# One order string for another: a recurrent attention block and a hard-swish layer on one core

## The chip, the cores and the metric

One core of a Trainium2 chip (trn2). The metric is the device time of one execution in microseconds. The engines are named as the profile names them: PE (TensorE, matrix products; PEld are its weight loads), DVE (VectorE), ACT (ScalarE), POOL (GpSimd) and SP (SyncE, which here issues nearly all DMAs).

## The reference

Two blocks behind each other. The first is a linear recurrence with 4 batches, 8 heads, 768 steps and head size 48; the second takes its result as 3072 tokens of width 384.

```
for t in range(S):
    cur = einsum('bhd,bhe->bhde', u * k[t], v[t])
    y[t] = einsum('bhd,bhde->bhe', r[t], state + cur)
    state = w[t][..., None] * state + einsum('bhd,bhe->bhde', k[t], v[t])
x = y.transpose(0, 2, 1, 3).reshape(3072, 384)
h = x @ w_in                              # 384 -> 2048
g = h * clip(h + 3, 0, 6) / 6
out = g @ w_out                           # 2048 -> 384
```

The weights `moe_w_in` and `moe_w_out` come as 64-bit floats and are turned into 32-bit ones on the chip.

## The kernel before

The sequence is cut into 24 chunks of 128 steps. Per chunk i, two scans on DVE (`back{i}`, `fore{i}`) make running products of the decay w; `K{i}` and `R{i}` scale k and r by them (on DVE for the first seven chunks, on POOL after); `own{i}`, `sum{i}` and `diag{i}` make the diagonal part with u (by PE's `dot{i}` for chunks below 9; from 9 on by two POOL multiplies, the second with u's broadcast over 128 partitions, and a DVE sum). `score{i}` multiplies K and R on PE, `above{i}` puts the causal half into A on DVE, `kv{i}` and `kvs{i}` make the new part of the state, `decay`, `mid`, `decb` and `state` update it on DVE, and `read{i}` gives the chunk's output, which `leave{i}` copies on ACT and `move` sets in place by DMA.

Four chunks make a block of 512 tokens; there are six. Block 0 runs its first product in plain form: `up0.f.c` on PE, `ramp` on ACT, `gate` on DVE. Meanwhile the weights are converted (`fetch` on SP, `low` and `sign` on ACT, `shift` and `full` on DVE) and the sums of weights for a scheme with fewer products are made on DVE (`sin`, `sout`). Blocks 1 to 5 use that scheme: sums of the input (`tx`), `up{b}.{d}.{r}` on PE, `read{b}...` on ACT and DVE, `clip`, `gate`. The second product of every block is done per half p as seven products `down{b}.{p}.{k}` in two parts each, with sums of g (`sum{b}.{p}`) ahead of them and reads of the banks (`out{b}.{p}.s1`, `u`, `v`, `c11`, `c12`, `c21`, `c22`) behind or between them, then `store`. Through blocks 1 to 5 the weights are fetched again and looked over (`refetch`, `vet`) for a flag at the end.

Everything is a step of a `Plan`: a name, an engine, a duration, what it comes after, the buffers that it holds. The order in which the steps are emitted, and so each engine's queue, is read from a string `ORDER`: two characters per step, its rank. The tile framework adds the waits that the data and buffers need; engines work off their queues in that order.

```
rank = [CODE.index(ORDER[2 * i]) * 64 + CODE.index(ORDER[2 * i + 1]) for i in range(len(steps))]
out = [n for _, n in sorted(zip(rank, steps))]
```

The plan also computes a start for each step from its durations. Its only use in the emitted program: where a PE step is to start later than PE would be free (in the first 60 us), `emit` puts filler matmuls (`spin`, L1276) in front of it; four more stand at the very beginning.

Other names of the profile: L397 is `fetch`, L354, L361 and L356 are the chunk loads (chunk 0 in two parts: `feat0`, `later`), L368 `tok` (v), L364 `u`, L373 `rkt` (r and k by token, from chunk 9), L713 `move`, L542 `flip` (a transposing DMA of K), L755 `store`, L434 and L438 `back`, L443 `fore`, L454 `K`, L458 `R`, L467 and L470 `own`, L479 `dot`, L739 `up0`, L840 `up` of the other blocks, L897 `down`, L917 the DVE reads of the banks, L816 `sout`, L787 to L791 `sin` and `tx`, L882 `sum`, L706 `leave`.

Of the kernel before, what the change touches and what calls it, by code (L numbers as in the profile page):

```python
# [81 lines left out]
ORDER = (
    "AEAIAHASATAVAKANAOAPAQARAbAjAXAYAZAaAhApAdAoAyA4A7AGALAeAmAiAsAlAWAcAtAuAvA+BCAwAxA8A9BDBPBHBIBMBdBiAfBhA1BKBNBQA6A2"
    "BEBFBJBpBzB0BLBVBnB1CBCJCLCNCeCkAgBYBTBlB7CKBfBRBoBtB4CaChCnB+CACSCWCMCpCrDYC3C5DTDBBjCOBwCsCqCtB3ByCHCfDJDLDUDfC7DD"
    "DRD0D3EDEIEPEVEzB5EUC6DMDaDgDIDADPDXEEEWEcDcD1EoEKFBFJFaFTFwHZG5CgFSDvECEvExD4ELElEyFPFQFhEhFmFWFrF0F/GmG1EXGUEmFiGD"
    "GRFZFbFjFlFvGHGtGFGMGbGpG9HBHFHKHcHdHfHxFRGfGSGZGzG7GYFnF4F9G6HeHtGkGlGoH9HSH/IBIgI1JqFUHMFVGjGuHjH5GnIXIoI+I/JBG4HY"
    "H7JcJsJtJuJvKkK4LELKHaKaJKH+JUJYKSJNJMJQKBKHLMJfKAKOKlKgKnKvLSLiHbK6HiJZKXK8LGJ5KbKuKzLILXK0K+LHLhLNLtLuLyL2MOL9IUJ+"
    "KeKyLYLkLqLBLmLnLsMBMCLeLfLgMdMeMfMuNQLCL7MRLzMFL5L/L1MjMmMxMyMzMGMUMYM7NCNDNwN3PyPvLdNTL8MpM+M6NZM0MqMrNLNkN5NNNRNn"
    "ONNqOQObOxO+PcM/NEN0NMNWNzOCNPOHOUPDPOPbNXN2OAPaO7PdPfPhPjQDQMQKNSOpOeNxOGPHPNN6PMPsP+P/QCO0PCPERWQ+RXRlRvRyScN1Q0PI"
    "PiP4QAQzP1QyQ3RPRQR2QBQIQnR5RFR7R8SQS/TmUBUCPlRxPwQiQxSASzQsRMRbTCTDTGSBSTSpTfS5TiTjTqT4UMQ4SISKRJSlTPTSRVSnSqTWTXUJ"  # L90
    "S7TITdUGTLUOUSUVUZUaUdUeSVTyTZTATsUDUPTNT+UXUoUpU3TtT6UAVQVRVZVaVdVoWuUQU6URUcUuUrVjUsUmUtUxVsVvU4U5VMVzVbV2WQWhW/Xe"
    "YMX1U0WXVHVIVkWPW+VKVlV7WNWfXFWZWzW0XZWGXbXrX3YJU7VrXaWHW2XTXhWkXfXmXpX2X7XHXOXYX+XMYBYCYWYeYxYjBgAFAJAkAnAqAzBWCTCU"
    "BcCbAMA0A5ArA/BXBZBmBrB2A3BABBBOBUCPCwCxCoDFAAABADACAUBkBvCEB6CRDrD7EOEQEaDCDlDnDwDyETEfEiEkE2E8E9FEE/FFFDFLFMFHFXB8"
    "CdDdC/DiD+EdEeEZErC+DWDjDmD/BSBaBbDpDtDxDqDzD2BGBeBsCCCcCiFAFOFgCjClCuDQDVDZEbEpEwC1C2C8CvCyCzEAEHEJCDCVCZE+FGFIDHDK"
    "DOESEYEnCXCYCmDsD5D6EMENERD9EFEGBqBuBxFpFuGLB/CFCQF7F8GODSDeDhEtE3E4DuD8EBEqEuE0B9CGCIEgEjEsDbDkDoE5E6E7C0C4DEGNGXGc"
    "C9DGDNGdGiGxFeFyF3GPGTGsG8G+HDHEHIHNHOHPHRHTHUHhHkHqHrHzH3H6IAIHIIILIPIeIhIiIkInIrI2I3I4I5I6I7JAFdFfFkFqGVGgF2GBE1GA"
    "FzF+FYGCF1GKFCFKFsFtFcFoF5F6GGGQGIGJGhGqFNFxGEGWGeGaG2HXIEGrHLG/HQGyHgHJHlGwG0GvHAHHHmHGHVHuHvHoHpH0H1G3HCHWHnHwHsH8"
    "IVINHyH2H4IJIKIbIpIyJSIZIlIxICISIsIDIMIYIGITIcIvIwI9IRIdIjIFIqIaImIuIQIOJEI8IWItIfIzI0JHJVJgJhJ0J7JGJXKiKjJkJ6LTLUJC"
    "JDJLJPJFJTJnJ1KKJpJxKCJaJbJ2JJJWJmJRJeJzJ/J4KGJIJlJoJOJrJwJyJ9JiJdKDKLJjKIJ3KJKFKPKQKRKUKhKoKVKWLDLWKEKMKtK/KNKTKsLA"
    "J8K3KfK1KcKdKwK9KZKmKYKpKrLFKxK2LQLRLLLOLZLaKqK5K7LJLvLPLrOfL+LVL4LwL6LjMELxMJLbLlLcLpMHMML3MAMIMNMKMLMbMhLoL0MDMPMa"  # L100
    "MVMkNAOgMQMSMcM8MlMvM3NJNgM5NFNcM4NaNlMTMiMsMWMgMwNGNKNdMtM2NfMZNIM1M9NHMnMXNUNeMoNmNBNbNVNhNjNuOIOLOYNoNyOMOnNYNiPr"
    "PtNONpPJPVN/OFOTOjOvOEOROlODOJOqNsN4N8NrN9OPOdOXOoOBOOOZNtOcOKOWOaN7NvOkOmN+OwOSOhOiOyOzO3O4PnPoOuO2PqP2OtO1PKPkOrOs"
    "P0P5OVO6PFPRO8PBPLPeO5O/O9PGPPPTPQPSPWPgPYPZPxPzPAPUPXP8PpPmQVT7TJP3QUQGQYP6QLQJQpP7P9QFQHQOQRQPQQQlQqQWQXQjQkQNQTQS"
    "QeQ5QhQmQ6SJQZQaQbQcQuQ/RERSRhRCRHRUR+R/ShQdQvQ8QfQwRBRLRGRYQ2RASSQtRRQ9RKRNQ1QgRTRaQ7SoRDRZRORgRqR3SDSCSYRdRkTHTURo"
    "RpTQTRRsR4TnTvRmRzR9SOSgSLSRSmStSuS0RfRnR1RcRtR0SUSPSaRuR6SyRiSNSFSGSZRrReSWSrRwS+SMSbSXSfSjSkSxT2T5S1S2TkTrSiSsTxTz"
    "SdSeTYTgSESHS9TOS3TMTBThSwS4SvS6TTTVTETFTbTuTcTeT3T9S8TKTaTlT1TpT/W7X0TwT0UNUhULUWUYUiUEUFUIUUUTUjUfUgUwU1UlUnUyUzUH"
    "UbUkUqU+UvU/VqWyU8U9VSVpVBVVVhVxWFWdWeWwVNVOVWVAVEVGVCVUVeVuVtV5VLVXVTVDVwVPVgWmVFVJWBWxVYVcVfV4V1V6WbXPXQWJWiX5X6Vn"
    "V3WaWcWIWKXqXyViV0V9WEWYW3XIXAXBXdWTWWWsV8WDWRVyWAWVWnWqW4WCWUWjV/WlWSWpXUWMV+XGXiWOWtWgWoWrW8XkXoYHXCXEYKYXW1W9YDYE"
    "XJXKYIYQWvW5YOYVYYY/YZYkYlYqYPYgYUYiYsYtYoYpZAZCYuYvY7Y9YhY5YrY4ZMY6ZEaFZxW6XVXcXwXLXsXgX4XRXSXWXXXnYFXtXuX8X9YRYSYa"
    "YbXjXlXvYGYmYTYfYwZwZTaEYzY0Y1Y2ZGZPZeZlZzZZZbZkaiala+Y3ZHZNY8ZJZQZiZhZnZKZSa2ZDZfZOZcZdZIZFZrZqZLbYZWZjZmZuZ0Z5aLau"  # L110
    "bAZ8aVbdbfaPaUbQbSZgZ1bHbPZRZ2aIaQagaHaOaXaxa5bRZyZ7Z6ZoaKaRafaYakZaZ4bDZ3aJZ+aNaSZ/Z9aTacaMbbaWahaZanaparasbmbnaeaj"
    "bcbpaoaqa3a/aaabbGbLadazawbEatbFbBbOaya4ama7a8bMa9bCbZbgbVbWbhbia6bUbKbTb8bXbtcEb9cDbubjbobsb+brbybxb1bkbqblbwb2b4bz"
    "b0cAcBb5b/cIcKbvb7b3b6cHcCcMcGcJcFcNQoQrZVZXToUKZpaAYyZBXNYAZUZYX/YcXzYNRIRjPuQEZsaBYnY+aDavT8U2YLYdaCa0ZtZvaGa1VmWL"
    "bIbJXDXxbNbabecL"
)
# [1509 lines left out]
```

## Time and profile before

| what | value |
|---|---|
| median of 3 runs | 528.02 us (526.06 to 531.23) |
| profiled execution | 528.87 us, its span 527.1 us |
| mean granted PE clock | 0.997 |
| PE busy | 517.7 us, 98% |
| DVE, ACT, POOL busy | 431.6, 290.1, 86.7 us |
| filler matmuls (L1276) | 94 instructions, 15.6 us |
| DMA | 70.33 MB, mean 133 GB/s |

Matmul ends are modelled and matmuls overlap, so the distance from one start to the next says more than a duration. A bracket behind a row gives the idle time of the engine before it and what ended it. A row of a stretch gives the busy time of each engine in it, with the count of instructions.

### The profile page before, as it was taken

The numbers are of one execution on the slowest core, as the hardware profiler recorded it, in microseconds if no ns is written. First come the engines' busy times: TensorE is split into PE (matmuls) and PEld (weight loads), VectorE is DVE, ScalarE is ACT, GpSimd is POOL, SyncE is SP. The second block draws the span as 40 slices with busy tenths as digits, with TensorE's granted clock in tenths as the row PEclk, the third lists the DMA queues.
The fourth block names the chain that finished last, engine by engine and source line by source line (L and its number), as shares of the span: only waits on it lengthen the run. The fifth ranks groups of instructions, "written<-read, shape, count | busy, mean of one in ns | idle before, by whom it ended". The sixth has DMA issues, their size and how long they took to land.

```text
span 527.1 us, 13608 instructions
## 1 busy us (share of the span) xinstructions
PE 517.7 (98%) x5642; PEld 477.7 (91%) x5642; DVE 431.6 (82%) x762; ACT 290.1 (55%) x680; POOL 86.7 (16%) x79
## 2 busy tenths in 40 slices
...
GB/s 329 329 275 182 234 285 92 49 53 181 150 3 63 54 172 68 96 206 72 109 99 101 150 10 130 140 101 106 265 33 153 101 151 203 131 199 136 60 10 57
DMA packets 37235, 70.33 MB, mean 133 GB/s; under 512 B 19088, under 2 KB 27184, under 8 KB 37168
## 3 DMA queue, kind: packets, MB, share of 16 engines
...
q8 instruction: 46, 0.75, 0.6%
...
q10 hardware_dynamic: 128, 0.00, 0.0%
HBM read 59.69 MB, written 4.72 MB: 122 GB/s over the span
## 4 chain that ended last, share of the span: by engine, by line
PE 86%; DVE 6%; DMA 3%; SPq 2%; ACT 1%; issue 1%; DVEq 0%
PE bank L897 29%; PE bank L840 28%; PE bank L739 8%; PE bankS L897 5%; PE bankS L840 5%; PE y_ps L598 2%; PE bank L504 2%; PE y_ps L607 2%; PE y_ps L620 2%; DMA feat_in<-in_feat_dram 1%; PE bankS L1276 1%; PE ps L479 1%; DMA bits<-in_moe_w_in_dram 1%; SPq L713 1%; DVE E L434 1%
## 5 line engine op out<-in xcount | busy, mean ns | idle before, releaser
L861 ACT ACTIVATE clip<-g,three 128x512 f32<-128x512 f32 x80 | 56.1, 719 | 49.0 <-DVE g L857 27.8
L857 DVE TENSOR_TENSOR g<-bank,g 128x512 f32<-128x512 f32 x80 | 53.4, 684 | 26.2 <-PE bank L840 23.1
L897 PE MATMUL bank<-w_out,g 128*128 128x192 f32 x384 | 67.3, 327 | 0.0
L897 PEld LDWEIGHTS bank<-w_out,g 128*128 128x128 f32 x384 | 63.2, 190 | 0.5
L865 DVE SCALAR_TENSOR_TENSOR g<-clip,g 128x512 f32<-128x512 f32 x80 | 59.1, 754 | 4.0 <-ACT clip L861 3.9
L495 ACT ACTIVATE A<-eyes,dg 128x64 f32<-128x64 f32 x192 | 49.8, 338 | 0.5 <-DVE dg L487 0.3
L454 POOL TENSOR_TENSOR K<-feat_in,E 112x512 f32<-112x512 f32 x17 | 25.0, 1469 | 146.0 <-DVE E L434 82.8
L855 ACT COPY g<-bank 128x512 f32<-128x512 f32 x50 | 28.8, 585 | 33.5 <-PE bank L840 32.3
L739 PE MATMUL bank<-xT,w_in 128*128 128x256 f32 (+1 forms) x216 | 46.7, 366 | 0.0
L739 PEld LDWEIGHTS bank<-xT,w_in 128*128 128x128 f32 x216 | 37.4, 194 | 4.5 <-issue 0.3
L458 POOL TENSOR_TENSOR W<-feat_in,W 112x512 f32<-112x512 f32 x17 | 25.3, 1490 | 94.4 <-DVE W L443 80.9
L840 PE MATMUL bank<-xT,w_in 128*128 128x256 f32 x160 | 40.1, 379 | 0.0
L706 ACT COPY xT<-y_ps 48x256 f32<-48x256 f32 x88 | 32.2, 365 | 10.4 <-PE y_ps L607 9.6
L915 ACT ACTIVATE o<-bank 128x192 f32<-128x192 f32 x36 | 11.5, 327 | 47.1 <-PE bank L897 47.0
L897 PE MATMUL bankS<-w_out,g 128*128 128x192 f32 x192 | 34.9, 328 | 0.0
L897 PE MATMUL bank<-more,g 128*128 128x192 f32 x192 | 34.4, 329 | 0.1
L840 PEld LDWEIGHTS bank<-xT,w_in 128*128 128x128 f32 x160 | 30.2, 190 | 3.8
L897 PEld LDWEIGHTS bank<-more,g 128*128 128x128 f32 x192 | 31.4, 190 | 1.1 <-DVE o L917 0.5
L434 DVE TENSOR_TENSOR_SCAN E<-feat_in,back 112x520 f32<-112x520 f32 x24 | 29.9, 1245 | 2.8 <-DMA feat_in<-in_feat_dram 2.8
L470 POOL TENSOR_TENSOR rk<-rk_in 128x384 f32<-128x384 f32 x15 | 17.5, 1164 | 88.9 <-DMA kvs<-rk 39.4
L897 PEld LDWEIGHTS bankS<-w_out,g 128*128 128x128 f32 x192 | 31.6, 190 | 0.2
L840 PE MATMUL bank<-xT,bits 128*128 128x256 f32 x120 | 30.7, 380 | 0.8 <-DMA xT<-xT 0.8
...
## 6 DMA issues: line engine op xcount, KB each, us to landing
...
bits<-in_moe_w_in_dram SPq DMA_DIRECT2D x8, 768.0 KB, 7.3
bits<-in_moe_w_out_dram SPq DMA_DIRECT2D x8, 768.0 KB, 5.6
feat_in<-in_moe_w_in_dram SPq DMA_DIRECT2D x8, 768.0 KB, 4.8
feat_in<-in_moe_w_out_dram SPq DMA_DIRECT2D x8, 768.0 KB, 4.5
...
v_in<-in_tok_dram SPq DMA_DIRECT2D x24, 192.0 KB, 4.4
feat_in<-in_wflat_dram SPq DMA_DIRECT2D x6, 768.0 KB, 4.7
```

The source lines that it names most:

```text
L434: nc.vector.tensor_tensor_scan(out=E_[:, ::-1], data0=d["w"][:, :0:-1], data1=back.rearrange("q p t -> q (p t)")[:, ::-1], initial=0.0, op ...
L454: early(i).tensor_mul(d["K"], d["k"], d["E"][:, :, 1:])
L458: early(i).tensor_mul(d["R"], d["r"], d["R"])
L495: nc.scalar.activation(out=d["A"][:, h, :], in_=eyes, func=ACT.Copy, scale=d["dg"][:, h])
L706: nc.scalar.copy(out=blocks[bk]["xT"][g * GP:g * GP + D, :, at:at + HL], in_=st[i]["y_ps"][a][(g ^ a) * GP:(g ^ a) * GP + D, :, :])
L739: nc.tensor.matmul(h_ps[:, :(c1 - c0) * L], lhsT=w_in[:, f // 2, j, f % 2, :], rhs=b["xT"][:, j, c0 * L:c1 * L], start=(j == 0), stop=(j = ...
L840: nc.tensor.matmul(b["p", d, c][:, z * HB:(z + 1) * HB], lhsT=weight(W_PLACE[r], d)[:, z, :], rhs=x_at(bk, X_PLACE[r]), start=fresh and z ...
L855: nc.scalar.copy(out=out_, in_=src)
L857: nc.vector.tensor_tensor(out=out_, in0=src, in1=out_of(bk, d, other), op=ALU.add if sign > 0 else ALU.subtract)
L861: nc.scalar.activation(out=c, in_=out_of(bk, d, u), func=ACT.Relu, bias=three, scale=twice)
L865: nc.vector.scalar_tensor_tensor(out=g, in0=blocks[bk]["r", d, u], scalar=6.0, in1=g, op0=ALU.min, op1=ALU.mult)
L897: nc.tensor.matmul(b["d", p, to][:, :h], lhsT=a, rhs=w(), start=(f == 0 and k in (1, 5)), stop=(f == HF - 1 and k in (2, 3, 4)), skip_grou ...
```

## The change

The string `ORDER` is replaced by another of the same length, a permutation of the same 1806 steps (459 on PE, 666 on DVE, 460 on ACT, 49 on POOL, 172 on SP). No step is added, taken away or altered, and no duration in the plan's table. The count of fillers follows from the order: 42 steps of two instructions instead of 47. What the reader will need of the two queues:

```
SP before    fetch6 feat0 later feat1 tok0 fetch0 tok1 fetch2 feat2 feat3 fetch4 fetch1 fetch3 tok3 u tok2 feat4 fetch7 ...
SP after     feat0 later feat1 tok0 fetch6 feat2 tok1 fetch0 fetch4 fetch3 feat3 tok2 fetch5 feat4 fetch1 fetch7 tok3 ...
             ... feat9 feat10 move1.0.1 move1.0.0 u rkt9 flip8 store0.0 move1.1.1 move1.1.0 ...

PE before    dot0 turn0 kv0 score0 dot1 clear0 first0 turn1 read0 kv1 score1 dot2 up0.1.0 clear1 first1 ...
             ... up0.15.2 down0.0.4.0 read6 down0.0.4.1 down0.1.5.0 down0.1.1.0 down0.1.1.1 down0.1.5.1
             down0.1.6.0 down0.1.2.0 down0.1.6.1 read7 (7 down steps) up1.0.12 up1.0.1 ...
PE after     dot0 turn0 kv0 dot1 turn1 score0 clear0 score1 kv1 dot2 first0 clear1 first1 turn2 read0 score2 read1 ...
             ... read6 down0.1.1.0 down0.1.1.1 down0.0.4.0 down0.1.2.0 down0.0.4.1 down0.1.5.0 down0.1.5.1
             read7 (9 down steps) up1.0.1 up1.0.9 ...

DVE before   ... sin0.4 sout4.0 out0.0.c22 gate0.14.2 out0.0.c12 ... tx1.0 ... sum9 ...
DVE after    ... out0.0.c12 sin0.7 sout4.0 sin0.8 sout4.1 sum0.1.1.0 fore8 out0.0.c22 sin0.9 above7 sin0.10 sum9
             sin0.11 ... sin0.20 sin1.0 tx1.0 ...

POOL before  K7 R7 K8 K9 R8 R9 own9 own10 ...
POOL after   K7 K8 R7 own9 R8 K9 R9 own10 ...
```

The diff, cut to its first lines (it goes on so through the whole string):

```diff
 ORDER = (
-    "AEAIAHASATAVAKANAOAPAQARAbAjAXAYAZAaAhApAdAoAyA4A7AGALAeAmAiAsAlAWAcAtAuAvA+BCAwAxA8A9BDBPBHBIBMBdBiAfBhA1BKBNBQA6A2"
...
+    "AAAIABAKALAZACAEAFAGAQAXAmArANAPATAUAWAcAnAwA/BIBZAHASAMAeAVAkAYARAaAdAgAlAoA9AfAjAsAxA5BBAyBABHBQBcAOBSAuA8BCBJA1Aq"
...
 )
```

More of the change, by code (lines that the diff above doesn't have):

```diff
@@ L82 @@
 ORDER = (
-    "AEAIAHASATAVAKANAOAPAQARAbAjAXAYAZAaAhApAdAoAyA4A7AGALAeAmAiAsAlAWAcAtAuAvA+BCAwAxA8A9BDBPBHBIBMBdBiAfBhA1BKBNBQA6A2"
-    "BEBFBJBpBzB0BLBVBnB1CBCJCLCNCeCkAgBYBTBlB7CKBfBRBoBtB4CaChCnB+CACSCWCMCpCrDYC3C5DTDBBjCOBwCsCqCtB3ByCHCfDJDLDUDfC7DD"
-    "DRD0D3EDEIEPEVEzB5EUC6DMDaDgDIDADPDXEEEWEcDcD1EoEKFBFJFaFTFwHZG5CgFSDvECEvExD4ELElEyFPFQFhEhFmFWFrF0F/GmG1EXGUEmFiGD"
-    "GRFZFbFjFlFvGHGtGFGMGbGpG9HBHFHKHcHdHfHxFRGfGSGZGzG7GYFnF4F9G6HeHtGkGlGoH9HSH/IBIgI1JqFUHMFVGjGuHjH5GnIXIoI+I/JBG4HY"
@@ L87 @@
[L87 to L111, printed above, removed]
@@ L112 @@
-    "bcbpaoaqa3a/aaabbGbLadazawbEatbFbBbOaya4ama7a8bMa9bCbZbgbVbWbhbia6bUbKbTb8bXbtcEb9cDbubjbobsb+brbybxb1bkbqblbwb2b4bz"
-    "b0cAcBb5b/cIcKbvb7b3b6cHcCcMcGcJcFcNQoQrZVZXToUKZpaAYyZBXNYAZUZYX/YcXzYNRIRjPuQEZsaBYnY+aDavT8U2YLYdaCa0ZtZvaGa1VmWL"
-    "bIbJXDXxbNbabecL"
+    "AAAIABAKALAZACAEAFAGAQAXAmArANAPATAUAWAcAnAwA/BIBZAHASAMAeAVAkAYARAaAdAgAlAoA9AfAjAsAxA5BBAyBABHBQBcAOBSAuA8BCBJA1Aq"
+    "AvA3A+BGBPBRBEBNBbBgBDBqByCnB+CRBKCMBTBwBiBsBkBLBVBmCICiCkCoB9CBCbCsCpC1C5DpC9DIDXDaBXCPCKC+CWC4CdCCCGCUClDTDnDqDGDS"
```

30 lines of the change are left out of this document (added).

## The prediction

> **What bounds the kernel now.** I read the page's parts 1 and 2 first, then stretches, waits, and the engines' rows in order of time.
>
> ```profile
> PE 517.7 (98%) x5642; PEld 477.7 (91%) x5642; DVE 431.6 (82%) x762; ACT 290.1 (55%) x680; POOL 86.7 (16%) x79
> ```
>
> PE is busy 98% of the span, but "busy" counts filler matmuls and half-speed ones. The stretches (columns: stretch, length, then busy us and count of PE, PEld, DVE, ACT, POOL, then granted clock, DMA share, GB/s):
>
> ```profile
> 0.00:8.33 8.33, 5.97 (x28) 5.78 (x28) 4.72 (x12) 3.32 (x4) 3.01 (x15) 1.00 0.75 279
> 5.66:30.00 24.34, 22.20 (x422) 20.36 (x421) 23.82 (x40) 20.70 (x57) 0.00 (x0) 1.00 0.93 356
> 30.00:60.00 30.00, 29.75 (x466) 25.48 (x459) 25.38 (x53) 24.77 (x63) 0.00 (x0) 0.94 0.57 202
> 60.00:95.00 35.00, 35.00 (x456) 30.96 (x456) 33.83 (x67) 28.05 (x67) 1.18 (x1) 1.00 0.57 195
> 95.00:129.50 34.50, 34.50 (x440) 33.11 (x439) 32.66 (x60) 16.05 (x40) 9.95 (x7) 1.00 0.37 98
> 129.50:132.83 3.33, 2.49 (x16) 2.19 (x15) 0.00 (x0) 0.70 (x2) 0.00 (x0) 1.00 0.47 156
> 134.78:523.75 388.97, 388.77 (x3836) 360.99 (x3836) 311.95 (x534) 198.21 (x450) 72.51 (x56) 1.00 0.36 111
> ```
>
> From 134.78 to 523.75 PE idles 0.20 us. No order can gain more than crumbs there, since both orders hold the same matmuls. So the case is block 0, up to 134.78. There DVE is as full as PE: it idles 0.52 + 4.62 + 1.17 + 1.84 + 3.33 = 11.5 us of the 127.2 from its first wait on data (5.66) to the first sum of block 1 (132.83), so 115.7 us are work. What PE lost in block 0 (the second fence line is the filler alone, by stretches of its source line: PE, PEld, clock, DMA, GB/s):
>
> ```profile
> 8.33 0.63 PE L479 MATMUL ps<-u_col,rk 112*64 112x2 f32 x16 [0.93 <-DVE rk L467]
> 8.33:60.00 51.67, 9.67 (x66) 8.61 (x66) 0.97 0.72 264
> 29.52 0.57 PE L620 MATMUL y_ps<-v_in,kn 64*48 64x48 f32 x32 [1.03 <-ACT xT L689]
> 30.77:34.18 3.41, 3.41 (x12) 2.81 (x11) 1.22 (x2) 0.67 (x4) 0.00 (x0) 0.50 0.99 403
> 132.52 1.10 PE L840 MATMUL bank<-xT,bits 128*128 128x256 f32 x4 [0.84 <-DMA xT<-xT]
> 134.78 1.10 PE L840 MATMUL bank<-T__1844,bits 128*128 128x256 f32 x4 [1.16 <-DVE T__1844 L787]
> ```
>
> The first real matmul comes at 8.33; filler takes 9.67 us after it; PE idles 1.03 at 28.5; a 3.41 us stretch runs at half clock (1.7 us of work lost); and at the seam to block 1 it waits 0.84 and 1.16.
>
> **Part by part.** The diff exchanges one order string: the same 1806 steps, durations unchanged. I decoded both strings into each engine's queue and matched the trace's instructions to the steps, so every step has a measured length (its start to the next start). Filler is placed by the planner: 47 filler steps before (94 instructions), 42 after; 10 instead of 14 ahead of the first real matmul, 32 instead of 33 behind it.
>
> **1, the start.** SP's first issues were a weight fetch, then chunk 0's decay part, then its rest; now the fetch stands behind chunk 1 and its v. (Issues, their times to landing, and the DVE instructions that they release:)
>
> ```profile
> 0.81 0.40 SPq L397 DMA_DIRECT2D bits<-in_moe_w_in_dram  x1
> 1.27 0.41 SPq L354 DMA_DIRECT2D feat_in<-in_feat_dram  x1
> 1.73 0.43 SPq L361 DMA_DIRECT2D feat_in<-in_feat_dram  x1
> bits<-in_moe_w_in_dram SPq DMA_DIRECT2D x1, 768.0 KB, 4.8
> feat_in<-in_feat_dram SPq DMA_DIRECT2D x1, 260.5 KB, 4.8
> feat_in<-in_feat_dram SPq DMA_DIRECT2D x1, 512.0 KB, 5.8
> 6.21 1.24 DVE L434 TENSOR_TENSOR_SCAN E<-feat_in,back 112x520 f32<-112x520 f32 x1
> 7.61 0.67 DVE L467 TENSOR_TENSOR rk<-feat_in 112x512 f32<-112x512 f32 x1
> ```
>
> Landings at 5.6, 6.1 and 7.5: after the first, 772 KB in 1.9 us, 400 KB/us. Issued first, chunk 0's 260 KB land (768 - 260) / 400 = 1.3 us sooner than the fetch did, at 4.35, and the rest at 5.7. DVE begins near 4.45 instead of 5.66: **1.2 us**; the first real matmul comes near 6.6. Bounds: 0 to 1.7.
>
> **2, the u broadcast and the order of fetches.** (Issue, times to landing of the v before it and of u, and DVE's wait:)
>
> ```profile
> 21.48 0.60 SPq L368 DMA_DIRECT2D v_in<-in_tok_dram  x1
> 22.12 0.43 SPq L364 DMA_DIRECT2D u_bc<-in_ub_dram  x1
> v_in<-in_tok_dram SPq DMA_DIRECT2D x1, 192.0 KB, 4.4
> u_bc<-in_ub_dram SPq DMA_DIRECT2D x1, 192.0 KB, 6.7
> 33.03 1.24 DVE L434 TENSOR_TENSOR_SCAN E<-feat_in,back 112x520 f32<-112x520 f32 x1 [2.19 <-DMA feat_in<-in_feat_dram]
> ```
>
> The v landed at 25.9, u at 28.8: 192 KB held the stream 2.9 us, against 0.5 at 400 KB/us. Chunk 4 stood behind u and six fetches. Now it stands behind five, and u behind block 1's first moves. By the landing chain chunk 4 comes near 27 instead of 33, so DVE's 2.19 goes. Next late there: the second score, which reaches PE near 24.5, behind six fillers (some 0.7 us of DVE idle). I followed PE, DVE and ACT through the first 30 us by hand with the rows' lengths: the step that ended at 34.5 (the one at half clock) ends near 29.8, with equal work done; DVE, idle 5.1 us to 60 before, should idle about 2.2. So DVE gains 1.2 + 2.9 = **4.1**, and PE, which from 60 on is tied to DVE by gates and sums (part 3), the same. Bounds: 1.5 (ACT, 83% busy from 30 to 60, paces DVE) to 5.5.
>
> **3, a new wait behind block 0's seventh output half.** The step `down0.0.4.0` must wait for `out0.0.c22`, which reads its bank. (DVE's c22; PE's `up0.15.2`, then `down0.0.4.0`:)
>
> ```profile
> 105.50 0.34 DVE L917 SCALAR_TENSOR_TENSOR o<-bank,o 128x192 f32<-128x192 f32 x1
> 104.82 1.46 PE L739 MATMUL bank<-xT,w_in 128*128 128x256 f32 x6
> 106.11 1.46 PE L897 MATMUL bank<-more,g 128*128 128x192 f32 x8
> ```
>
> Before, c22 started at 105.50 after 93.6 us of DVE work (steps added up, from 0), so DVE ran 11.9 behind its work; down0.0.4.0 started at 106.11 after 83.6 us of PE work, 22.5 behind. The difference of **10.6** hardly moves from 60 on, as each engine waits for the other when it does. Now c22 comes after 100.8 us, down0.0.4.0 after 88.1: with c22's 0.27 and 0.15 to get there, the difference must be 13.1. PE would arrive 2.5 us early; behind it wait all of block 0's remaining matmuls, and DVE's sum of `down0.1.5.1` then waits 2 us for PE. Some of PE's usual small gaps vanish in that wait: net **1.8 lost**. [...]
>
> **4, GpSimd in the busy stretch.** `own9` (two instructions) ran while DVE idled; now it stands ahead of R8, near 105, when DVE is full. (POOL and DVE rows:)
>
> ```profile
> 103.31 1.44 POOL L454 TENSOR_TENSOR K<-feat_in,E 112x512 f32<-112x512 f32 x1 [1.57 <-DVE E L434]
> 103.63 1.94 DVE L816 TENSOR_TENSOR more<-w_out,top 128x768 f32<-128x768 f32 x1
> 126.33 1.18 POOL L470 TENSOR_TENSOR rk<-rk_in 128x384 f32<-128x384 f32 x1
> 89.26 0.95 DVE L816 TENSOR_TENSOR top<-w_out,bits 128x768 f32<-128x768 f32 x1
> ```
>
> A sum that takes 0.95 elsewhere (last row) took 1.94 beside a POOL multiply: it ended 0.8 after that multiply's end, 104.75. So each POOL instruction can cost DVE up to 1; two here, 0 to 2, of which the K multiplies, moved to earlier places, give about 1 back at c22. [...]
>
> **5, the seam to block 1.** Its first sum needs read7's outputs moved by DMA. Before, 7 matmul steps of 1.30 us followed read7, now 9: 2.6 us more cover for copy, moves and sums, against 0.84 + 1.16 us of waits and 0.4 around them. They go: **2.4 gained** (bounds 0.5 to 2.5).
>
> **6, behind.** In block 1 one gate stands 0.7 us too late for `down1.0.1.1` (queue positions); blocks 2 to 5 have the old margins. **0.6 lost** (0 to 1.2).
>
> Sum: -4.1 + 1.8 - 2.4 + 0.6 = **-4.1**, on the profiled 528.87 (span 527.1 and 1.8 around it): 524.8. The median shown is 528.02, 0.85 lower, its runs 526.06 to 531.23. I forecast 528.0 - 4.1, rounded: **524.0**.
>
> **Rivals.** [...]
>
> *Given back*: ACT and DVE hold each other through two clip buffers from 30 to 60, so part 2 gives 1.5, and PE falls to half clock once (1.7, of which 1.0 hides behind DVE): -1.5 + 1.8 - 2.4 + 0.6 + 0.7, near 527.2. The row for the clock: PE idled 1.03 us in the 3.4 before 30.77 and half clock followed; filler is thinner now. [...]
>
> *Slower: u comes too late.* u is issued only when leave5 has let two moves go, then rkt9; own9 waits for both, R8 waits behind own9 on POOL, read7 needs R8, and DVE's `sum9` now stands ahead of half of block 1's weight sums. (A leave's four copies, and one move's three issues:)
>
> ```profile
> 122.42 1.51 ACT L706 COPY xT<-y_ps 48x256 f32<-48x256 f32 x4 [1.64 <-PE y_ps L607]
> 52.16 1.87 SPq L713 DMA_DIRECT2D xT<-xT  x3
> ```
>
> The value copy ahead of leave5 on ACT waits for down0.0.5.1, which ends after 74.5 us of PE work, near 92.7; plus 1.5, plus two moves, u is issued near 98.5 and lands 5 to 6.7 later, near 104; rkt9 1 us behind; own9 (2.2) ends near 107. sum9's turn is at 102.4 us of DVE work, near 111. From 112 every microsecond of lateness is one of span; from 116 the kernel is slower than before; at 120 it takes 532. Against: it needs 9 us of error.
>
> **How the numbers follow.** Forecast 524.0: 0.47 (522.7 to 525.8). All arrives, 521: 0.24. Given back, 527.2: 0.22. Slower, 530 and more: 0.07. Range 520.3 to 528.2, leaving out some 0.06 below and 0.1 above. One per cent is 5.3 us, about what a measurement can tell. Faster by over 1% is under 522.7: 0.24 and a little of the forecast's, 0.28. Slower by over 1%: 0.04. Within: 0.68.
>
> **What would show it.** The first scan near 4.5 and first L479 near 6.6; no 2.19 wait of DVE on feat_in near 30; clock 1.0 there; a PE wait on `o` or a DVE gap of about 2 us near 107 to 117; no wait on xT or T at the seam, block 1's first sums' matmuls near 130 instead of 134.8; from there to the end 389 us again. Wrong if sum9 waits for POOL, or DVE's idle time to 60 stays near 5.

## The result, and the profile after

The changed kernel takes 526.06 us (median of 22 runs, 521.57 to 528.43) against 528.29 for the one before (526.06 to 531.31): a ratio of 0.9946, 95% interval 0.9925 to 0.9967. The forecast was 524.0. The profiled execution took 525.09, 3.8 below the profiled one of before, where the sum said 4.1. Several of the sum's terms were wrong, though, by up to 2.4 us, and they cancel. The medians differ by 2.2, the ratio makes it 2.8: the profiled execution ran at a mean granted clock of 1.000, which only 4 of the 22 runs did, 17 of them at 0.994 to 0.998 (one stretch of 3.41 us at half clock, as in the profiled execution of before from 30.77 to 34.18, makes the mean 0.0033 less and costs at most 1.7 us). The profiled execution of before, on the other side, held that one, so up to 1.7 of the 3.8 is the clock of two single executions. All ratios and the medians of the experiments leave out the few runs that are over 1.5% above the fastest of their kernel (one each of e3, e4 and e9, at 534.1, 760.4 and 595.9 us, and three of before).

First the page of the changed kernel, busy time and instructions of each engine:

```profile
PE 513.0 (98%) x5632; PEld 475.7 (91%) x5632; DVE 430.5 (82%) x762; ACT 292.4 (56%) x680; POOL 83.4 (16%) x79
```

Then the stretches that answer to those of before (stretch, length, busy us and count of PE, PEld, DVE, ACT, POOL, granted clock, DMA share, GB/s):

```profile
0.00:6.03 6.03, 4.13 (x21) 3.94 (x21) 4.23 (x11) 1.49 (x2) 3.01 (x15) 1.00 0.69 246
4.40:30.00 25.60, 24.15 (x470) 21.76 (x470) 23.40 (x40) 20.68 (x60) 0.00 (x0) 1.00 0.88 336
30.00:60.00 30.00, 29.75 (x435) 25.80 (x434) 28.93 (x60) 28.13 (x72) 0.00 (x0) 1.00 0.71 245
95.00:126.94 31.94, 31.94 (x429) 31.18 (x429) 30.52 (x64) 9.61 (x31) 6.43 (x5) 1.00 0.22 63
145.17:149.57 4.40, 2.25 (x132) 2.02 (x131) 3.29 (x8) 0.58 (x1) 1.09 (x1) 1.00 0.52 208
126.94:518.43 391.49, 389.22 (x3842) 362.24 (x3840) 311.79 (x530) 202.13 (x450) 68.98 (x56) 1.00 0.37 114
```

From 30 to 60 DVE is busy 28.93 instead of 25.38 us, at full clock. Block 1's first sums' matmuls come at 126.94 (134.78 before), with no idle time of PE ahead of them. But from there on PE idles 2.27 us (391.49 - 389.22), nearly all of it in the fifth row's 4.4 us. PE's rows in order of time:

```profile
6.03 0.63 PE L479 MATMUL ps<-u_col,rk 112*64 112x2 f32 x16 [0.47 <-DVE rk L467]
126.94 1.03 PE L840 MATMUL bank<-T__1846,bits 128*128 128x256 f32 x4
149.22 0.42 PE L607 MATMUL y_ps<-A,v_in 64*48 64x64 f32 x10 [2.15 <-issue]
```

"issue" means that PE waited for nothing that the profile shows. This gap, in the middle of a reading (`read8`), was in no term of the sum. The other surprise is the tail: PE's last matmul ends at 518.43, the span at 523.3, so 4.9 us, against 523.75 and 527.1, 3.35, before.

**Where the time went, for all kernels.** As in the prediction, "behind" is PE's time less the matmul work done up to there (steps added up, filler left out; the least value in the ten us from the time named). All from the one profiled execution of each, but for the ratio. e9 to e11 ran on another chip than e1 to e8, the kernel before beside them on both.

| kernel | behind at 60 | 120 | 150 | 500 | last matmul ends | tail | ratio to before (95%) |
|---|---|---|---|---|---|---|---|
| before | 21.3 | 23.1 | 26.2 | 30.6 | 523.75 | 3.4 | 1 |
| after | 17.6 | 18.8 | 21.5 | 25.5 | 518.43 | 4.9 | 0.9946 (0.9925 to 0.9967) |
| e1 loads moved | 17.6 | 18.8 | 19.1 | 23.0 | 515.90 | 4.8 | 0.9890 (0.9864 to 0.9915) |
| e2 last stores | 16.8 | 18.0 | 20.2 | 24.0 | 516.88 | 3.4 | 0.9906 (0.9874 to 0.9937) |
| e3 u early | 18.1 | 19.3 | 21.5 | 25.3 | 518.18 | 5.0 | 0.9924 (0.9900 to 0.9948) |
| e4 own9 early | 17.0 | 18.2 | 18.5 | 22.3 | 515.25 | 5.0 | 0.9940 (0.9915 to 0.9965) |
| e5 = e1 + e2 | 20.8 | 22.0 | 22.2 | 26.1 | 519.01 | 3.4 | 0.9847 (0.9819 to 0.9876) |
| e6 seam | 17.8 | 19.7 | 20.0 | 24.0 | 516.85 | 5.0 | 0.9955 (0.9933 to 0.9977) |
| e7 before, u late | 18.7 | 20.5 | 21.8 | 26.4 | 519.28 | 3.6 | 0.9975 (0.9953 to 0.9997) |
| e8 e7 + new start | 18.9 | 20.9 | 22.9 | 27.8 | 520.74 | 3.7 | 0.9977 (0.9954 to 0.9999) |
| e9 e5, c22 late | 18.7 | 20.8 | 21.1 | 25.0 | 517.86 | 3.3 | 0.9910 (0.9878 to 0.9943) |
| e10 e5, old start | 20.5 | 22.2 | 22.4 | 26.3 | 519.21 | 3.4 | 0.9920 (0.9891 to 0.9949) |
| e11 e10, u early | 23.4 | 25.4 | 25.5 | 29.6 | 522.54 | 3.4 | 0.9949 (0.9923 to 0.9974) |

The column at 60 scatters, first of all with the clock at the start. e5's profiled execution ran 6.83 us at half clock there, twice the 3.41 of before, where e1's ran at full clock:

```profile
9.36:16.19 6.83, 6.81 (x70) 6.50 (x71) 6.02 (x11) 4.42 (x13) 0.00 (x0) 0.50 0.91 373
```

```profile
9.36:16.19 6.83, 6.81 (x118) 6.04 (x122) 6.75 (x14) 6.61 (x19) 0.00 (x0) 1.00 0.97 364
```

PE got 70 matmuls done instead of 118, and e5 is 3.2 us further behind at 60 with the same queue. Some 0.7 of that it had lost ahead of this stretch (the 31st matmul of the data began at 9.59, at 8.86 in e1), so 3.41 us at half clock cost some 1.3 to 1.6 us. e10 has 3.42 us of half clock up to 60 (mean granted clock 0.997), e11 twice that (0.993), before 3.41 (0.997), the others none. It scatters at full clock, too: the changed kernel, e1, e2, e4, e6 and e9 have the same queues up to 60 and lie between 16.8 and 18.7. A difference of less than 2 us in this column shows nothing by itself.

### The profile page after: what moved, and what is told of

Same layout as the page of the kernel before. It is cut to its first block, busy times and chain, and to the rows that moved or that the text cites. A ratio compares the mean times of both kernels' runs of the same rounds, so it can differ in the third digit from the quotient of the medians.

```text
span 523.3 us, 13600 instructions
## 1 busy us (share of the span) xinstructions
PE 513.0 (98%) x5632; PEld 475.7 (91%) x5632; DVE 430.5 (82%) x762; ACT 292.4 (56%) x680; POOL 83.4 (16%) x79
## 4 chain that ended last, share of the span: by engine, by line
PE 97%; issue 1%; DMA 1%; DVE 0%; ACT 0%; DVEq 0%
PE bank L897 36%; PE bank L840 28%; PE bank L739 8%; PE bankS L897 6%; PE bankS L840 5%; PE y_ps L598 3%; PE bank L504 2%; PE y_ps L607 2%; PE y_ps L620 2%; PE bankS L1276 2%; PE ps L479 1%; PE ps L520 1%; DMA feat_in<-in_feat_dram 1%; PE bank L682 0%; PE y_ps L682 0%
## 5 line engine op out<-in xcount | busy, mean ns | idle before, releaser
L861 ACT ACTIVATE clip<-g,three 128x512 f32<-128x512 f32 x80 | 56.2, 718 | 40.4 <-DVE g L857 21.3
L857 DVE TENSOR_TENSOR g<-bank,g 128x512 f32<-128x512 f32 x80 | 54.0, 686 | 22.8 <-PE bank L840 19.7
L739 PE MATMUL bank<-xT,w_in 128*128 128x256 f32 (+1 forms) x216 | 44.7, 359 | 0.0
L470 POOL TENSOR_TENSOR rk<-rk_in 128x384 f32<-128x384 f32 x15 | 17.8, 1188 | 136.0 <-DMA kvs<-rk 89.7
L706 ACT COPY xT<-y_ps 48x256 f32<-48x256 f32 x88 | 32.1, 365 | 10.6 <-PE y_ps L607 9.8
L458 POOL TENSOR_TENSOR W<-feat_in,W 112x512 f32<-112x512 f32 x17 | 21.9, 1289 | 74.1 <-DVE W L443 55.0
L443 DVE TENSOR_TENSOR_SCAN W<-feat_in,start 112x520 f32<-112x520 f32 x24 | 30.2, 1258 | 1.2 <-PE ps L643 1.2
L434 DVE TENSOR_TENSOR_SCAN E<-feat_in,back 112x520 f32<-112x520 f32 x24 | 29.6, 1234 | 0.5 <-DMA feat_in<-in_feat_dram 0.5
```

The costliest lines, as they stand in the source:

```text
L434: nc.vector.tensor_tensor_scan(out=E_[:, ::-1], data0=d["w"][:, :0:-1], data1=back.rearrange("q p t -> q (p t)")[:, ::-1], initial=0.0, op ...
L443: nc.vector.tensor_tensor_scan(out=W_, data0=d["w"][:, :-1], data1=starts[i % 2].rearrange("q p t -> q (p t)"), initial=0.0, op0=ALU.mult, ...
L706: nc.scalar.copy(out=blocks[bk]["xT"][g * GP:g * GP + D, :, at:at + HL], in_=st[i]["y_ps"][a][(g ^ a) * GP:(g ^ a) * GP + D, :, :])
L739: nc.tensor.matmul(h_ps[:, :(c1 - c0) * L], lhsT=w_in[:, f // 2, j, f % 2, :], rhs=b["xT"][:, j, c0 * L:c1 * L], start=(j == 0), stop=(j = ...
L857: nc.vector.tensor_tensor(out=out_, in0=src, in1=out_of(bk, d, other), op=ALU.add if sign > 0 else ALU.subtract)
L861: nc.scalar.activation(out=c, in_=out_of(bk, d, u), func=ACT.Relu, bias=three, scale=twice)
```

## Experiments on the two losses that the sum lacked

**e1, the gap of 2.15 us.** The changed kernel's SP queue, with two chunk loads moved:

```
- ... tok10 rkt10 store0.2 tok9 store0.3 flip9 feat11 feat12 flip10 ...
+ ... tok10 rkt10 feat11 feat12 store0.2 tok9 store0.3 flip9 flip10 ...
```

> The changed kernel with the loads of chunks 11 and 12 (feat11, feat12) issued right behind rkt10, near 123, instead of behind flip9, near 141. Theory: TensorE's 2.15 us of idle at 147.05 is a wait for the next 16 KB piece of its own program, which came over the DMA engines at 146.79, right behind chunk 11's landing at 146.47. With both loads landed by about 131 the piece comes before TensorE needs it: no idle of more than 0.3 us from 140 to 155, and a time 2.1 us below the changed kernel's, a ratio to before near 0.9905. Rival 1: the idle is a wait inside the reading (a decay or a buffer) that the profile does not name: it stays within 0.3 us of 2.15 and the ratio stays near 0.9946. Rival 2: the piece's wait only moves to another place: the gap is gone here and one of 1 us or more stands elsewhere behind 100.

Measured: 522.61 us (521.63 to 523.28), ratio 0.989. The view of DMA queues shows what matters, cut to short windows. In the changed kernel, from 141.00 to 146.70 (queue, kind: packets, MB, share of 16 engines):

```profile
q1 hardware_dynamic: 1159, 1.56, 85.7%
```

and from 146.70 to 147.80:

```profile
q1 hardware_dynamic: 52, 0.24, 55.4%
q8 instruction: 1, 0.02, 5.2%
```

The page has `q8 instruction: 46, 0.75, 0.6%`: 46 packets of 16 KB; the counts below say that they are PE's own program. While the two loads moved 1.56 MB the view lists no other queue, so none of these got through; the one that PE needed left at 146.79, right behind chunk 11's landing (146.47), landed at 147.71, and PE went on 1.5 us later. In e1 PE is at the same place (`read8` at 145.19 against 145.17), and the packet comes between 140.80 and 142.30, at 140.87; the reading runs through, and no gap of 1 us stands elsewhere:

```profile
q8 instruction: 1, 0.02, 5.7%
```

```profile
146.59 0.65 PE L607 MATMUL y_ps<-A,v_in 64*48 64x64 f32 x30
147.16 1.13 PE L840 MATMUL bank<-T__1846,bits 128*128 128x256 f32 x4
```

More facts say the same. The gap stands also in e2 and e3, which leave these loads in place; there the packets landed at 146.23 and 147.59, and PE went on 1.64 and 1.58 later:

```profile
147.87 0.42 PE L607 MATMUL y_ps<-A,v_in 64*48 64x64 f32 x10 [1.59 <-issue]
```

```profile
149.17 0.42 PE L607 MATMUL y_ps<-A,v_in 64*48 64x64 f32 x10 [1.59 <-issue]
```

The changed kernel has one more such gap, in the crowded early stream, behind a packet that landed at 21.06:

```profile
22.55 0.42 PE L607 MATMUL bank<-A,v_in 64*48 64x64 f32 x11 [0.78 <-issue]
```

1.5 us behind the landing again, and 3328 of PE's instructions ahead of the other gap, 13 times 256; 13 packets landed from behind 21.06 to 147.71. e11, whose early stream is another, has its gap 256 of PE's instructions behind the place of that one, 1.48 us behind a packet that landed at 31.29:

```profile
32.77 0.29 PE L620 MATMUL y_ps<-v_in,kn 64*48 64x48 f32 x2 [1.35 <-issue]
```

And in e4 the gap is gone though both loads stand where they did: there the packet left at 140.27, half a microsecond before chunk 11's load was issued. (e4, DMA queues from 140.00 to 140.60, then SP's row.)

```profile
q8 instruction: 1, 0.02, 13.3%
```

```profile
140.79 1.62 SPq L356 DMA_DIRECT2D feat_in<-in_feat_dram  x2
```

In e6, too, there is no gap: the packet left at 142.15, 0.1 us before the load was issued. So it is a race of half a microsecond or less between PE's next piece of program and a load, and the stretch of `read8` above holds 132 matmuls and 131 weight loads in 2.25 us of PE, about as many instructions as one packet's 256. In the changed kernel PE waits ("issue") behind two of the 46 packets, 0.78 and 2.15 us. e1's median gains 3.4 us on the changed kernel's, PE's last matmul 2.5. In e11 PE ran at half clock from 33.70 to 37.11, 0.9 us behind the gap's end; behind the gaps near 147 of the changed kernel, e2 and e3 the clock stayed at 1.0. Whether the gap brought on e11's half clock is not shown.

**e2, the tail.** DVE's `out5.0.c12` two steps earlier, and SP's last stores in another order:

```
- DVE  sum5.1.3.1 out5.1.c22 out5.1.c12 out5.0.c12
+ DVE  sum5.1.3.1 out5.0.c12 out5.1.c22 out5.1.c12
- SP   store5.2.e store5.3.e store5.0.e store5.2 store5.1 store5.1.e store5.0 store5.3
+ SP   store5.0.e store5.1 store5.1.e store5.0 store5.2.e store5.3.e store5.2 store5.3
```

> The changed kernel with the last stores in another order: out5.0.c12 right behind sum5.1.3.1 on VectorE (near 509 instead of 516), and the stores of chunk 0's outputs issued first, so that only store5.2 and store5.3 are left behind 516. Theory: the 4.9 us from TensorE's end to the span's end (3.4 before) hold 0.45 us of SyncE still issuing store5.0 and 1.05 us of a last landing among three others. Then the tail is 3.3 to 3.6 us, the last landing takes 1.6 us, and the time falls by 1.4 us, a ratio to before near 0.992. Rival: the tail is the scatter of one execution: it stays at 4.5 us or more, or is as short without a change of the time.

Measured: 522.52 us (522.05 to 526.11), ratio 0.9906; tail 3.4. The end of the changed kernel, by time, and its last store by time to landing (from 519.20 on), then e2's:

```profile
517.76 1.83 SPq L755 DMA_DIRECT2D out_dram<-o  x2
...
518.46 0.33 ACT L915 ACTIVATE o<-bank 128x192 f32<-128x192 f32 x1 [7.47 <-PE bank L897]
```

```profile
out_dram<-o SPq DMA_DIRECT2D x1, 96.0 KB, 2.7
```

```profile
out_dram<-o SPq DMA_DIRECT2D x1, 96.0 KB, 1.6
```

ACT's last read ends at 518.79, but SP is busy with the store before until 518.84, issues the last one at 519.26, and this lands among three others in 2.7 us; in e2 in 1.6. The 1.5 us were the order of the last stores. The median fell by more, 3.5; e2's profile began 0.8 better and its gap was 0.56 shorter, neither of them its edit's, and where the rest of the median's gain comes from is not shown.

**e5, both.** The edits of e1 and e2 in one kernel.

> The changed kernel with the edits of e1 (loads of chunks 11 and 12 behind rkt10) and of e2 (last stores) together. Theory: two separate losses, so the savings add: no idle of TensorE over 0.3 us from 140 to 155, TensorE's last matmul ends near 516 and the tail is 3.4 us, a span near 519.4 and a ratio to before of 0.984 to 0.988, below each of the two alone (0.989 and 0.9906). Rival: the two medians near 522.5 are one and the same gain (e2's profile was 0.8 us early at the start and its idle 0.56 us shorter, neither of them its edit): then the ratio stays at 0.989 to 0.991.

Measured: 520.70 us (520.12 to 524.13), ratio 0.9847, below either alone: two losses, and they add. No gap over 0.3 us from 140 to 155, tail 3.4. The profiled execution was the slowest of the six (524.13), by the half clock shown above. This is the fastest version of all.

## Experiments on the first 60 us

**e3, u back in the stream of the changed kernel.**

```
- SP  ... feat3 tok2 fetch5 feat4 ...     ... move1.0.0 u rkt9 flip8 ...
+ SP  ... feat3 tok2 u fetch5 feat4 ...   ... move1.0.0 rkt9 flip8 ...
```

> The changed kernel with u's broadcast back in the early stream, right behind tok2 and ahead of fetch5 and feat4. By the prediction's second step the broadcast takes 2.4 us of the stream: chunk 4 lands near 29 instead of 26.46, everything of the stream behind it is later too, and TensorE and VectorE are about 2 us later at 60 (offsets near 19.6 and 9); time 2 us above the changed kernel's, ratio near 0.998. Rival: in the new order chunk 4 is scanned only at 38.0, 11.5 us behind its landing, so the broadcast could have stayed: offsets at 60 within 0.3 us of the changed kernel's, ratio near 0.9946.

Measured: 524.30 us, ratio 0.9924; no loss in the median, and 0.5 behind the changed kernel at 60, which lies within that column's scatter. Chunk 4 landed at 28.0, 1.5 later than in the changed kernel, and its scan waited for nothing in either. The rival holds: in the new order chunk 4 is scanned late enough for u to have stayed. The changed kernel's DVE row (no wait in it; chunk 4 landed at 26.46):

```profile
38.01 1.23 DVE L434 TENSOR_TENSOR_SCAN E<-feat_in,back 112x520 f32<-112x520 f32 x1
```

**e7, u late in the kernel before**, one step moved:

```
- SP  ... fetch3 tok3 u tok2 feat4 ...   ... feat9 rkt9 flip7 ...
+ SP  ... fetch3 tok3 tok2 feat4 ...     ... feat9 rkt9 u flip7 ...
```

> The kernel before with one edit: u's broadcast issued behind rkt9 instead of behind tok3 in the early stream. Theory (step 2 alone): chunk 4 lands 2.4 to 2.9 us earlier, near 30.3, VectorE's wait of 2.19 us before back4 at 33.03 goes, and TensorE is 2 us earlier from 35 on; ratio near 0.996. Rival: other work sets TensorE's pace from 30 to 60 (its own queue, ScalarE, the half clock from 30.77 to 34.18), so the wait goes and TensorE gains 0.5 us or less; ratio 0.999 to 1.001.

Measured: 526.43 us (524.70 to 529.60), ratio 0.9975 (0.9953 to 0.9997). Chunk 4 landed at 30.11 (32.91 before), and its scan waits for nothing:

```profile
30.61 0.28 DVE L750 SCALAR_TENSOR_TENSOR g<-clip,bank 128x128 f32<-128x128 f32 x1
30.81 1.24 DVE L434 TENSOR_TENSOR_SCAN E<-feat_in,back 112x520 f32<-112x520 f32 x1
```

2.6 us ahead at 60 in the profile, of which up to 1.6 is the half-clock stretch that before's profiled execution had and this one had not; 1.3 us (0.2 to 2.5) in the ratio. So the step's mechanism is there in the old order: the landing and the wait as the theory has them, the gain at its low end, with an interval that reaches into the rival's.

**e8, the new start too**: e7, with SP's `feat0 later feat1 tok0` ahead of `fetch6`, and the first steps of DVE, ACT and PE (through `shift6`, `diag11`, `turn1`) in the changed order.

> The kernel before with the start of the changed one on every engine (SyncE: feat0, later, feat1, tok0 ahead of fetch6; VectorE, ScalarE and TensorE in the changed order through shift6, diag11 and turn1, the rest as before) and u's broadcast behind rkt9. Theory (steps 1 and 2 are what the changed kernel gains until 60): first scan near 3.9, first matmul of the data near 6.0, TensorE 3.5 to 4.1 us earlier at 60, and with the seam as before a ratio near 0.993. Rival 1: the stream's landings alone set the time at 60, so this is as far ahead as u's move alone. Rival 2: the rest of the old order, written for later landings, waits elsewhere until 60 and keeps less than 1.5 us.

Measured: 526.37 us, ratio 0.9977. The first matmul of the data came at 5.97, 2.4 us ahead of e7's; `read0` (L682) came at the same time in both, behind filler. (PE's rows of e8, then e7.)

```profile
18.47 1.16 PE L1276 MATMUL bankS<-ident 128*128 128x128 f32 x8
19.46 1.23 PE L682 MATMUL y_ps<-xT,S__117 112*128 112x64 f32 x10
```

```profile
18.01 1.60 PE L1276 MATMUL bankS<-ident 128*128 128x128 f32 x12
19.45 1.23 PE L682 MATMUL y_ps<-xT,S__117 112*128 112x64 f32 x10
```

The lead is gone within 14 us, and DVE's rows show two waits that took it. DVE's first step began 1.8 earlier in e8, and at the scan of chunk 2 (18.72 against 18.70) it is level again: in between it waited for the landing of chunk 1 and for ACT.

```profile
8.54 1.24 DVE L434 TENSOR_TENSOR_SCAN E<-feat_in,back 112x520 f32<-112x520 f32 x1 [0.87 <-DMA feat_in<-in_feat_dram]
...
17.84 0.96 DVE L421 CUSTOM_DVE_ANT_0 w_in<-top,more 128x1536 uint16<-128x1536 uint16 x1 [0.61 <-ACT more L411]
```

On PE `score0`, which the new start puts behind `turn1`, began at 14.33, 2.0 later than in e7. The scan of chunk 2 waits for no landing in either. So the theory fails, and both rivals have a share in it: one wait is for a load, the other for a step in the rest of the order.

**e10 and e11, the old start in the new order**: e5 with `fetch6` put ahead of `feat0` again, and then u behind `tok2` as well.

```
- SP  feat0 later feat1 tok0 fetch6 feat2 ...
+ SP  fetch6 feat0 later feat1 tok0 feat2 ...
```

> The kernel of e5 with the first fetch back in its old place: fetch6 ahead of feat0 on SyncE (the planner then puts five filler matmuls more ahead of the first real ones). Undoes the landings of the prediction's first step in the new order. Theory (step 1 pays through to the end): feat0 lands near 6.1 instead of 3.75, first scan near 6.2, first matmul of the data near 8.3 instead of 6.0, and TensorE 1.2 to 2.3 us later at 60 and at the end; median 522 to 523. Rival, from e8, where the new start in the old order gave nothing: something later in the stream sets the pace, and by 60 the loss is 0.5 us or less; median within 0.6 us of 520.7.

> The kernel of e10 with u's broadcast, too, back in the early stream, behind tok2 as in e3. Theory (steps 1 and 2 as summed): by 60 TensorE is 3.5 us or more behind the changed kernel's, median near 524.5. Rival: the order of the compute steps alone, with chunk 4 scanned at 38 instead of 33, covers most of either: 60 is reached 1.5 us or less later than in the changed kernel and the median is below 522.5.

Measured: e10 524.49 us (522.65 to 525.65), ratio 0.992, 3.8 above e5; e11 525.35 (523.36 to 527.64), another 0.9. Here the start pays. Part of the 3.8 is clock: 7 of e10's 12 runs had a mean clock of 0.997 or less, 1 of e5's 6. The runs at 1.000 alone differ by 2.9 (523.3, three runs, against 520.4, four). Against e9 on the same chip (522.5, five runs; see below) e10 is 0.8 slower, and e9 holds a wait of 0.9 that e10 doesn't have: 1.7. The column at 60 holds 3.42 us at half clock for e10, twice that for e11, so its 2.9 and 5.8 on e1 are some 1.3 to 1.6 and 2.6 to 3.2 without them, within the scatter or near it. So the start is worth nothing that shows in the old order and some 2 to 3 us in the new one, u's place 1.3 and 0 to 0.9; the two figures for u are not clear of the noise.

## Experiments on the end of block 0

**e4, own9 ahead of c22.**

```
- SP  ... feat10 move1.0.1 move1.0.0 u rkt9 flip8 ...
+ SP  ... feat10 u rkt9 move1.0.1 move1.0.0 flip8 ...
```

> The changed kernel with u and rkt9 issued ahead of move1.0.1 and move1.0.0, near 94 instead of 99, so that own9's three multiplies run on GpSimd near 99 to 102 instead of 105.0 to 107.6, ahead of the output step out0.0.c22. By the prediction's third step they hold VectorE back by about 2 us there: c22 ends near 107.5 instead of 105.9, the sums' matmuls down0.0.4.0 stand still for 1 to 1.8 us behind 106.57, and block 1's first matmul up1.0.1 comes near 128.3 instead of 126.94; time about 1.4 us above the changed kernel's if nothing gives it back. Rival: GpSimd's multiplies cost VectorE nothing at this place: c22 stays near 105.6, TensorE runs through, up1.0.1 within 0.3 us of 126.94 and the time the same.

Measured: 525.36 us, ratio 0.994. It did not test what it was to test: u and rkt9 landed at 97.70 and 98.50, but own9 (two multiplies, not three) then waited until 103.4. The bracket names PE's reading, but no step of own9 in the kernel waits for one. It waits for `flip8`: own9 writes the buffer `rk` that flip8's transposing DMA reads, and this was issued at 100.41 and landed 2.9 later.

```profile
103.59 2.31 POOL L470 TENSOR_TENSOR rk<-rk_in 128x384 f32<-128x384 f32 x1 [17.47 <-PE y_ps L607]
```

So it began 1.4 earlier than in the changed kernel, not 5, and `c22` (105.01) was as much earlier as all of e4 is. For the 1.4 us that own9 ran ahead of c22 it was POOL's multiply that took longer (2.31 us instead of 1.41), and DVE's steps took as long as in the changed kernel. That speaks for the rival as far as it goes; the 5 us of the theory were not tried.

**e9, c22 behind own9.** e5, with c22 moved on DVE:

```
- DVE  ... fore8 out0.0.c22 sin0.9 above7 sin0.10 sum9 ...
+ DVE  ... fore8 sin0.9 above7 sin0.10 out0.0.c22 sum9 ...
```

> The kernel of e5 with one more edit: the output step out0.0.c22 three steps later on VectorE, behind sin0.10, so that it stands behind own9's multiplies on GpSimd. This makes by hand the wait that the prediction's third step forecast (1.8 us at down0.0.4.0). Theory: TensorE goes through its queue in order, so what it waits there it keeps: down0.0.4.0 starts 1.4 to 2.2 us later against read6 than in e5, up1.0.1 is as much later, and the median is 1.4 to 2.2 us above e5's 520.7 (ratio to before near 0.988). Rival: block 1 has room to take it back (its sums and gates run ahead of TensorE): the wait is there, the median within 0.5 us of e5's.

Measured: 523.08 us, ratio 0.991. The wait of the prediction's third step, made by hand:

```profile
108.53 1.57 PE L897 MATMUL bank<-more,g 128*128 128x192 f32 x8 [0.69 <-DVE o L917]
```

From 60 to 120 PE falls 2.1 behind instead of 1.2, and keeps the 0.9 to the end (6.3 from 60 to 500, e1 5.4). The wait is paid in full; it was only shorter than expected, since c22 ends 0.67 before PE comes (105.90 against 106.57 in the changed kernel), and this went first. The median's 2.4 above e5 is more than the profile accounts for; the two ran on different chips.

**e6, two groups back.**

```
- PE  ... down0.1.5.1 read7 down0.1.6.0 down0.1.6.1 down0.1.2.1 ...
+ PE  ... down0.1.5.1 down0.1.6.0 down0.1.6.1 read7 down0.1.2.1 ...
```

> The changed kernel with the reading read7 two matmul groups later on TensorE (behind down0.1.6.0 and down0.1.6.1), so that seven of block 0's groups stand behind it, as in the kernel before, instead of nine. By the prediction's fifth step it is these two groups, 2.6 us, that cover the wait at the seam: TensorE then waits again before block 1's first sums' matmuls, 2.0 to 2.4 us in all. Rival: most of the old wait came from SyncE, where the moves stood behind the loads of chunks 10 and 11 and took up to 6.7 us to land; in the new queue they land within 1.2 us of their issue and VectorE's tx1.0 ends at 124.88, 2.06 us before up1.0.1 needs it: then 2.6 us later costs 0.4 to 0.7 us only.

Measured: 526.49 us, ratio 0.9955. PE waits 0.44 for a bank, and for nothing at the seam:

```profile
119.95 2.87 PE L897 MATMUL bank<-w_out,g 128*128 128x192 f32 x16 [0.44 <-ACT o L915]
...
127.86 1.03 PE L840 MATMUL bank<-T__1846,bits 128*128 128x256 f32 x4
```

Seven groups cover the way, too. What made the difference were the moves, by time to landing: of before, the last but one (issued at 124.58 behind two chunk loads on SP), then of the changed kernel the last one (issued at 119.64).

```profile
xT<-xT SPq DMA_DIRECT2D x3, 16.0 KB, 6.3
```

```profile
xT<-xT SPq DMA_DIRECT2D x3, 16.0 KB, 1.8
```

6.3 us against 1.8 (1.8 in e6 too). The moves of before stood behind `feat10` and `feat11`; the new queue has no load near them. So the changed queues cover the way without the two groups. DVE's order there differs too, but before DVE idled 3.33 us up to 132.83, when the last moves (issued from 127.10, 4.9 to landing) were in; whether the two groups alone would have done was not tried.

## Why the prediction was right, and where it was not

1. **The start** was mis-sized. Forecast 1.2 us on DVE and 1.7 on PE; the first scan came at 3.85 instead of 6.21 and the first matmul at 6.03, 2.3 earlier. The step read the landing from 260 KB at the stream's speed behind the fetch; issued first, they landed 2.9 us from issue. By e10 the start is worth 2 to 3 us, with the seam's 2.9 the larger parts of the gain.

```profile
3.85 1.27 DVE L434 TENSOR_TENSOR_SCAN E<-feat_in,back 112x520 f32<-112x520 f32 x1 [0.49 <-DMA feat_in<-in_feat_dram]
```

2. **u and the fetches.** Chunk 4 at 26.46 (27), no wait on it, clock 1.0: as said, and the sum of steps 1 and 2, 4.1, came out as 3.7 at 60. Up to 1.6 of this is the half-clock stretch of before's execution. The step counted its end as gained; yet the mean clock of 17 of the changed kernel's 22 runs (0.994 to 0.998) says that such stretches stay in most of them (these figures don't say where), which is a part of the rival Given back. So the 3.7 agrees better than the mechanism deserves. The share of u was wrong: in the new order, by e3 and e11, 0 to 0.9, since the scan of chunk 4 moved from 33 to 38. Taking a row of the old order as the price of an edit in the new one was the failure; only the landing carried over.

3. **The new wait: 0 instead of 1.8.** This is the term that failed most. c22 ran at 105.56, the group at 106.57 without a wait:

```profile
106.57 1.46 PE L897 MATMUL bank<-more,g 128*128 128x192 f32 x8
```

"The difference of 10.6 hardly moves" was the broken sentence: it was 13.6 here (PE 18.4 behind, DVE 4.8). DVE's step lengths were taken from before, and two of them hold time beside POOL's multiplies: the sum of 1.94 took 0.96 now, `sin0.5` 0.42 instead of 1.40. The prediction saw this ("give about 1 back at c22") and left it out of its 1.8; it was 2 of the 3 us by which the difference moved. (Before's `sin0.5`, then the changed kernel's sum.)

```profile
109.17 1.40 DVE L791 TENSOR_TENSOR bits<-w_in 128x256 f32<-128x256 f32 x1
```

```profile
101.73 0.96 DVE L816 TENSOR_TENSOR more<-w_out,top 128x768 f32<-128x768 f32 x1
```

4. **POOL near 105**: own9 at 105.03, as said. It does slow DVE, to 0.91 and 0.55 for sums of weights of which the like takes 0.41, and R8 behind it slows the next one to 0.94: some 1.2 us in all, but behind c22, where PE doesn't wait for DVE. (POOL's rows of own9 and R8, then DVE's.)

```profile
105.03 1.41 POOL L470 TENSOR_TENSOR rk<-rk_in 128x384 f32<-128x384 f32 x1 [18.35 <-DMA kvs<-rk]
106.52 1.06 POOL L471 TENSOR_TENSOR rk<-rk,u_bc 128x384 f32<-128x384 f32 x1
107.54 1.36 POOL L458 TENSOR_TENSOR W<-feat_in,W 112x512 f32<-112x512 f32 x1
```

```profile
105.81 0.91 DVE L791 TENSOR_TENSOR T__1537<-w_in,bits 128x256 f32<-128x256 f32 x1
...
107.31 0.55 DVE L789 TENSOR_TENSOR T__1537<-bits,w_in 128x256 f32<-128x256 f32 x1
107.78 0.54 DVE L487 TENSOR_REDUCE dg<-rk 128x8 f32<-128x384 f32 x1
108.25 0.94 DVE L789 TENSOR_TENSOR T__1537<-apart,w_in 128x256 f32<-128x256 f32 x1
...
109.72 0.41 DVE L789 TENSOR_TENSOR w_in<-T__1537,w_in 128x256 f32<-128x256 f32 x1
```

Each of these three sums ended 0.28 or 0.29 behind the end of the multiply that it met (106.72 and 106.44, 107.86 and 107.58, 109.19 and 108.90), and so did before's `sin0.5` (110.57 and 110.29). In these four cases, then, DVE paid for what was left of the multiply when the sum came: 0.64 of own9's 2.5 us (0.50 and 0.14 over the 0.41 of the like), where the prediction's step allowed up to 2; and the sum of the forecast lost nothing by it.

u landed at 103.0 (104 forecast), but own9 waited 2 us longer, for flip8's transposing DMA (the first POOL row); that it ended near 107 as forecast is luck. The rival with u too late was nearer than it looked: `sum9`'s turn came at 107.78 (the row L487), not 111, and own9 had ended at 107.58, 0.2 before.

5. **The seam**: 2.4 forecast, and the waits are gone (2.9 in "behind", 23.1 to 26.0 before). The cause named, nine groups instead of seven, was not needed (e6). The step left out the moves' way through SP: 4.9 to 6.3 us to landing before, 1.8 to 3.1 now.

6. **Block 1**: 0.6 forecast at a gate; there is no loss at that gate, and 2.15 at the reading instead, a wait for PE's program that no step of the prediction had.

The sum by the table, forecast in brackets: to 60, -3.7 (-4.1); from 60 to 120, -0.6 (+1.8); the seam, -2.9 (-2.4); block 1 to 150, +2.5 (+0.6); from there to PE's end, -0.6 (0); the tail, +1.5 (none): -3.8 (-4.1). What came out worse adds up to 3.8 (0.4, 1.9, 1.5), what came out better to 3.5 (2.4, 0.5, 0.6): that the total is right is luck in part. And -3.8 compares two single executions; by the ratio of all runs the gain is 2.8. The 521 that had a chance of 0.24 was not reached (526.06): there was no wait behind c22, but block 1 lost 2.5.
